# Local attention with a gated convolution: the first half pair divided behind its values, its queries and keys in four loads

## The chip, the core and the metric

The kernel runs on one core of a Trainium2 chip. Five engines work side by side, each through its own list in order: TensorE (PE, matrix products; PEld is its loading of weights), VectorE (DVE), ScalarE (ACT), GpSimd (POOL) and SyncE (SP), which here issues all transfers. The metric is device time in microseconds, the median of several runs; a profile shows one execution, with a span (first to last instruction) inside that execution's time.

## The reference

Attention within chunks of 64 positions, 8 heads of 64, then a gate: a causal convolution of five taps over the result, a sigmoid, times a projection, and a second projection.

```
scores = (q_c @ k_c.T) / 8                      # per chunk of 64
attn = exp(scores - max); attn = attn / (sum(attn) + 1e-9)
x = (attn @ v_c)  -> (8, 576, 512)
gate = sigmoid(sum over k of conv_w[k] * x shifted by 4 - k)
out = (gate * (x @ w_val)) @ w_out
```

All is 32 bits wide: q, k, v are 8 x 8 x 576 x 64, the two weights 512 x 512.

## The kernel before, in words

The 4608 positions are cut into 9 groups of 512 (g = 0 to 8). The 8 heads of a group are two pairs (p = 0, 1) of four heads each. A pair's scores are 64 small products of TensorE (`S`), into one bank of its accumulators; VectorE takes the max of each row (`mx`) and subtracts it (`sb`), ScalarE takes the exponential (`ex`), VectorE the sum and its reciprocal (`sm`), GpSimd divides (`nm`), TensorE transposes (`T`), ScalarE copies (`ec`), TensorE multiplies with the values (`A`), and ScalarE copies the result, x, with channels as partitions (`xc`). Pair 1 of group 0 has its max subtracted by TensorE (`mh`, `ml`, `sp`, then `ep`), and some pairs let ScalarE subtract it (`ng`, `ea`, `rc`).

x is then split in a rounded part (`xr`) and a residual (`xd`), so that three fast products make one exact enough (`V`, for 4 blocks m of outputs and 4 quarters c of the inputs). The weights are split likewise on the chip: they come as bits, and clamp, scale, sign, merge, shift, add, round and residual are the pieces `w1`, `w2`, `w3`, `w4`, `w5`, `w7`, `w6`, `wb` for the value weights `v` and the output weights `o`. The first products of group 0 use unsplit weights and x (`F`, two slow passes each). The taps are `k0` and `k` (VectorE mostly), the gate `sg`, its product `gm` or `vc` and `gs`, the split of it `gr` and `gd`, the second projection `P`, the copy out `oc`, the store `st`.

The order of everything is one written list, `ORDER`: a piece a word, `name group ...`. Each engine runs its share of this list in that order. A letter behind a name puts a piece on another engine (D VectorE, G GpSimd). `SLOTS` gives each tile its buffer: `ld` has six for q, k and v, `acc` four (raw weights and convolution sums), `ps` and `big` the accumulators. A piece waits for the last reader of its buffer.

Pair 0 of group 0 is in `BY_HALF`: its heads go in two halves (the third number, 0 or 1), so that the second half's scores run while the first is in the softmax. Before, the whole q and k of that pair are loaded in two transfers of 512 KB, and the division of each half (`nm 0 0 0`, `nm 0 0 1`) stands on GpSimd ahead of the half's transposes. `W` is a run of products with a zero tile, whose result nobody reads.

Of the kernel before, what the change touches and what calls it, by code (L numbers as in the profile page):

```python
# [16 lines left out]

ORDER = """lk 0 0,lq 0 0,lc,lw v 0,zr 0,w1G c 0,zw,lk 0 1,S 0 0 1,mx 0 0 1,S 0 0 0,zi,sb 0 0 1,mx 0 0 0,ex 0 0 1,zr 1,lq 0 1,
w5 v 0,sb 0 0 0,lw v 2,W 5,sm 0 0 1,w1G v 0,nm 0 0 1,w3 c 0,zm,ex 0 0 0,w5 c 0,S 0 1 0,w2 v 0,sm 0 0 0,lv 0 0,S 0 1 1,
w3 v 0,lw v 1,mx 0 1,w3 v 2,lk 1 0,nm 0 0 0,w1G v 2,w5 v 2,w2 c 0,hl 0,lq 1 0,w4 v 0,w4 c 0,T 0 0 0,w7 v 0,ec 0 0 0,  # L20
T 0 0 1,w1 v 1,mh 0 1,w9,A 0 0 0,w2 v 2,xc 0 0 0,lw o 3,w3 v 1,ml 0 1,w2 v 1,sp 0 1,ep 0 1,F 0 2 0,lw v 3,ec 0 0 1,
w4 v 2,lq 1 1,w4 v 1,k0 0 0,w7G v 2,w6 v 2,F 0 3 0,F 0 1 0,sm 0 1,w5 v 1,w7G v 1,A 0 0 1,lv 0 1,S 1 0 0,w1G v 3,
xc 0 0 1,w3G o 3,k 0 0 1,w6 v 0,nmD 0 1,lk 1 1,S 1 0 1,F 0 0 0,T 0 1,mx 1 0,k0 0 1,w5 o 3,F 0 1 1,lw o 0,w5 v 3,
w3 v 3,w1G o 3,F 0 3 1,sb 1 0,ec 0 1,ex 1 0,wb v 2,A 0 1,w2 v 3,k 0 0 4,k 0 0 2,xc 0 1 1,sm 1 0,w1G o 0,xc 0 1 0,
S 1 1 0,w3 o 0,lk 2 0,lq 2 0,xr 0 1,nm 1 0,S 1 1 1,F 0 2 1,k0 0 2,lw o 2,xn 0 1,xe 0 1,mx 1 1,sb 1 1,F 0 0 1,ex 1 1,
w4 v 3,V 0 2 2,V 0 1 2,w7G v 3,k 0 2 3,w5 o 0,sm 1 1,S 2 0 0,S 2 0 1,w3G o 2,w2 o 3,w6 v 3,T 1 0,w6 v 1,ec 1 0,mx 2 0,
V 0 0 2,lk 2 1,V 0 3 2,lq 2 1,lv 1 0,wb v 3,k 0 2 2,lv 1 1,S 2 1 0,sb 2 0,k 0 0 3,S 2 1 1,w2 o 0,ex 2 0,mx 2 1,nm 1 1,
A 1 0,V 0 0 3,k0 0 3,V 0 3 3,xr 1 0,sm 2 0,wb v 0,xc 1 0 1,sb 2 1,vc 0 3,V 0 1 3,V 0 2 3,xc 1 0 0,T 1 1,w1G o 2,
xd 1 0,ex 2 1,V 1 3 0,ec 1 1,sm 2 1,lk 3 0,lq 3 0,vc 0 1,S 3 0 0,S 3 0 1,nm 2 0,k 0 1 2,lw o 1,w2 o 2,wb v 1,A 1 1,
sg 0 0,nm 2 1,xc 1 1 0,V 1 3 1,mx 3 0,lv 2 0,gm 0 0,V 1 1 0,xc 1 1 1,hl 1,lk 3 1,ng 3 0,k 0 2 1,w1G o 1,lk 4 0,  # L30
V 1 1 1,V 1 2 0,xr 1 1,V 1 2 1,xd 1 1,V 1 3 2,w4 o 2,V 1 2 2,V 1 1 2,V 1 3 3,k 0 3 2,V 1 1 3,k 0 2 4,w4 o 0,k 0 1 3,
ea 3 0,k 0 3 4,k 0 1 1,w2 o 1,vc 1 3,T 2 1,lq 3 1,w3G o 1,T 2 0,vc 1 1,rc 3 0,k 0 3 3,w4 o 1,ec 2 0,V 1 0 0,V 1 0 1,
ec 2 1,w5 o 1,S 3 1 0,S 3 1 1,k 0 3 1,A 2 0,V 1 0 2,V 1 2 3,sg 0 2,w5 o 2,k 0 1 4,lq 4 0,mx 3 1,xr 2 0,vc 1 2,w7G o 1,
lv 2 1,sb 3 1,lq 4 1,ex 3 1,V 1 0 3,sg 0 3,k0 1 1,A 2 1,xd 2 0,w4 o 3,V 2 2 0,V 2 3 0,vc 1 0,xc 2 0 0,xc 2 0 1,lq 5 0,
w7 o 0,V 2 3 1,V 2 0 0,gm 0 2,V 2 2 1,V 2 0 1,xr 2 1,lv 3 1,lk 4 1,S 4 0 0,k0 1 2,nm 3 0,sm 3 1,S 4 0 1,gs 0 3,w6 o 1,
xd 2 1,gr 0 2,V 2 2 2,mx 4 0,k0G 1 0,sg 0 1,w7G o 2,k 1 1 3,V 2 0 2,V 2 0 3,w6 o 2,gr 0 0,gs 0 1,gdD 0 0,xc 2 1 0,
xc 2 1 1,sb 4 0,V 2 3 2,w6 o 0,V 2 1 0,w7G o 3,V 2 1 1,w6 o 3,k 1 0 1,S 4 1 0,nm 3 1,S 4 1 1,mx 4 1,k 1 0 4,gr 0 1,
gd 0 2,T 3 1,k 1 1 1,V 2 1 2,k 1 2 2,lv 3 0,vc 2 0,ec 3 1,wb o 0,ng 4 1,wb o 1,k 1 1 4,gdD 0 1,V 2 2 3,lk 5 1,k0 1 3,
k 1 2 3,V 2 1 3,P 0 2 0,vc 2 2,wbD o 2,P 0 1 0,hl 2,k 1 2 1,vc 2 1,k 1 0 3,V 2 3 3,k 1 3 4,k 1 1 2,k 1 3 1,P 0 0 0,
ea 4 1,P 0 0 1,rc 4 1,P 0 2 1,lq 5 1,vc 2 3,P 0 2 2,lk 5 0,P 0 0 2,wbD o 3,k 1 3 3,ex 4 0,T 3 0,k 1 2 4,P 0 1 1,  # L40
ec 3 0,P 0 3 0,A 3 1,k 1 3 2,A 3 0,P 0 3 1,xr 3 1,gr 0 3,k 1 0 2,xr 3 0,xc 3 0 0,sm 4 0,P 0 3 2,xc 3 0 1,P 0 1 2,
gd 0 3,sg 1 3,xcD 3 1 0,P 0 1 3,P 0 0 3,P 0 2 3,xc 3 1 1,sg 1 0,P 0 3 3,xd 3 0,oc 0 1,S 5 0 0,S 5 0 1,oc 0 0,oc 0 2,
xd 3 1,oc 0 3,S 5 1 0,S 5 1 1,V 3 3 0,gs 1 0,V 3 0 0,V 3 2 0,nm 4 1,gr 1 0,k0G 2 2,V 3 0 1,V 3 0 2,V 3 3 1,V 3 2 1,
V 3 0 3,sg 1 2,mx 5 0,V 3 3 2,mx 5 1,V 3 1 0,V 3 1 1,sb 5 0,k0 2 3,nm 4 0,T 4 0,ng 5 1,V 3 2 2,k0 2 1,V 3 2 3,V 3 3 3,
sg 1 1,ea 5 1,T 4 1,vc 3 0,vc 3 3,ec 4 0,gs 1 1,gr 1 1,gd 1 0,P 1 3 0,hl 3,lk 6 0,P 1 2 0,V 3 1 2,k 2 3 2,k 2 2 1,
V 3 1 3,k 2 1 3,lq 6 0,gs 1 2,gr 1 2,k0 3 1,lv 5 0,S 6 0 0,S 6 0 1,ec 4 1,k0G 2 0,k 2 2 2,k 2 0 4,lv 5 1,gs 1 3,
k 2 2 4,lv 4 0,gr 1 3,k 2 0 1,st 0 0,k 2 3 4,vc 3 2,lk 7 1,lv 4 1,vc 3 1,A 4 0,k 2 0 3,P 1 0 0,k 2 1 1,k 2 3 1,rc 5 1,
gdD 1 1,k 2 0 2,P 1 1 0,k 2 1 2,k 2 1 4,k 2 2 3,k0 3 3,sg 2 0,mx 6 0,P 1 2 1,k0 3 0,ex 5 0,k 2 3 3,gd 1 3,k0 3 2,
P 1 0 1,gd 1 2,P 1 1 1,P 1 3 1,sm 5 0,P 1 0 2,sg 2 1,P 1 1 2,nm 5 1,sg 2 2,P 1 2 2,sg 2 3,xr 4 0,gs 2 0,P 1 0 3,
sb 6 0,xd 4 0,k 3 0 2,gs 2 1,P 1 3 2,P 1 1 3,lq 6 1,lk 6 1,P 1 2 3,xc 4 0 0,xc 4 0 1,S 6 1 0,S 6 1 1,oc 1 2,k 3 2 1,  # L50
oc 1 0,k 3 0 1,gr 2 1,gr 2 0,A 4 1,V 4 2 0,nm 5 0,P 1 3 3,xr 4 1,ocD 1 1,V 4 0 0,k 3 3 4,V 4 2 1,st 0 2,hl 4,mx 6 1,
# [607 lines left out]
```

## Time and profile before

| | us |
|---|---|
| median of 3 runs (lowest, highest) | 265.33 (265.31, 266.5) |
| the profiled execution | 267.69 |
| its span | 265.9 |
| busy: TensorE, VectorE, ScalarE, GpSimd | 251.2, 236.3, 188.6, 103.3 |

Busy time is an average over stages with different limits, and a product's end is modelled: a busy TensorE still may wait in it. All instructions of the kernel go through one helper, so that one source line stands for all; groups are told apart by their tiles. `big` holds scores, transposes and values, `ps` the projections, `acc` raw weights and convolution sums, `x` the attention's result, `rs` sums and reciprocals, `t` and `t2a` and so on are scratch.

### The profile page before, as it was taken

Reading aid. Unit: us, or ns where it says so; the run is one execution under the profiler, and the core shown is the slowest. Engines: PE = TensorE matmul, PEld = TensorE weight load, DVE = VectorE, ACT = ScalarE, POOL = GpSimd, SP = SyncE. Lnnn points to the kernel's source line nnn. Section 1 sums busy time; section 2 is a strip of 40 time slices with the busy share of each in tenths; the row PEclk is TensorE's granted clock in tenths of the full one; section 3 lists DMA queues with packets and bytes.
Section 4 is the critical chain, followed back from the end, with each engine's and each line's share of the span. In section 5 each row is a group of like instructions: output and inputs, shape, how many; then the busy total and the mean of one; then the engine's idle time right before and its main releaser. Section 6 shows DMA issues by size and latency. Waiting matters only on the chain. (4 is left out here: it accounts for less than half of the span.)

```text
span 265.9 us, 7860 instructions
## 1 busy us (share of the span) xinstructions
PE 251.2 (94%) x3314; PEld 213.7 (80%) x3315; DVE 236.3 (89%) x329; ACT 188.6 (71%) x440; POOL 103.3 (39%) x90
## 2 busy tenths in 40 slices
...
GB/s 226 402 416 395 360 391 273 81 147 179 212 103 147 155 218 20 262 163 78 83 198 31 247 1 188 172 79 2 2 205 192 2 41 4 197 0 0 81 276 158
DMA packets 14291, 42.47 MB, mean 160 GB/s; under 512 B 1712, under 2 KB 1712, under 8 KB 14256
## 3 DMA queue, kind: packets, MB, share of 16 engines
...
q8 instruction: 26, 0.43, 0.7%
q14 instruction: 9, 0.07, 0.1%
HBM read 32.53 MB, written 9.44 MB: 158 GB/s over the span
## 5 line engine op out<-in xcount | busy, mean ns | idle before, releaser
L158 DVE SCALAR_TENSOR_TENSOR acc<-x,cw,acc 128x516 f32<-128x516 f32 (+1 forms) x144 | 106.2, 780 | 1.2 <-ACT acc L158 0.8
L158 PE MATMUL ps<-t,v_hi 128*128 128x512 f32 x240 | 82.3, 389 | 0.0
L158 PEld LDWEIGHTS ps<-t,v_hi 128*128 128x128 f32 x240 | 45.2, 189 | 7.1 <-issue 0.2
L158 PE MATMUL ps<-t,v_lo 128*128 128x512 f32 x120 | 45.6, 380 | 0.0
L158 PE MATMUL ps<-o_hi,t 128*128 128x512 f32 x124 | 44.3, 382 | 0.1
L158 PEld LDWEIGHTS big<-ld,ld 64*64 64x64 f32 x1152 | 19.4, 139 | 12.5 <-issue 10.7
L158 PE MATMUL big<-ld,ld 64*64 64x64 f32 x1152 | 21.8, 226 | 7.6 <-DMA ld<-in_q 7.1
L158 POOL TENSOR_TENSOR t<-e_row,rs 128x1024 f32<-128x1024 f32 (+1 forms) x13 | 25.1, 1933 | 8.1 <-DVE rs L158 6.5
L158 DVE TENSOR_REDUCE mx<-big 128x16 f32<-128x1024 f32 (+1 forms) x19 | 21.8, 1153 | 7.1 <-PE big L158 6.9
L158 PEld LDWEIGHTS ps<-o_hi,t 128*128 128x128 f32 x124 | 23.4, 189 | 3.8 <-DVE t2o L158 0.5
L158 ACT COPY x<-big 128x512 f32<-128x512 f32 (+3 forms) x44 | 19.4, 497 | 9.2 <-PE big L158 5.0
L158 PEld LDWEIGHTS ps<-t,v_lo 128*128 128x128 f32 x120 | 22.7, 189 | 3.0 <-issue 0.2
L158 ACT ACTIVATE acc<-x,cw 128x516 f32<-128x516 f32 (+1 forms) x27 | 19.9, 745 | 0.1
L158 ACT ACTIVATE t<-acc 128x512 f32<-128x512 f32 (+7 forms) x35 | 15.6, 505 | 5.9 <-DVE acc L158 2.8
L158 PE MATMUL ps<-o_lo,t 128*128 128x512 f32 x52 | 19.7, 379 | 0.0
L158 ACT ACTIVATE e_row<-big,mx 128x64 f32<-128x64 f32 x64 | 19.1, 363 | 0.6 <-DVE mx L158 0.6
L158 ACT ACTIVATE e_row<-e_row 128x1024 f32<-128x1024 f32 (+1 forms) x14 | 14.0, 1012 | 7.0 <-DVE e_row L158 7.0
L158 PEld LDWEIGHTS big<-t,ld 64*64 64x64 f32 x960 | 15.8, 135 | 3.9 <-issue 1.8
L158 PE MATMUL big<-t,ld 64*64 64x64 f32 x960 | 17.5, 220 | 1.0 <-issue 0.7
L158 ACT ACTIVATE t<-big 128x1024 f32<-128x1024 f32 x13 | 13.4, 1035 | 7.0 <-PE big L158 6.9
L158 DVE TENSOR_REDUCE rs<-e_row 128x16 f32<-128x1040 f32 (+1 forms) x15 | 17.4, 1157 | 0.2
L158 ACT CAST t<-big 128x1024 fp32r<-128x1024 f32 x16 | 16.5, 1033 | 1.2 <-PE big L158 1.2
...
## 6 DMA issues: line engine op xcount, KB each, us to landing
...
```

The source lines that it names most:

```text
L158: return tc.keep_in_program_order(fn(*args, **kwargs))
```

## The change

- q and k of the first pair come in four transfers of 256 KB, `lq 0 0 0`, `lk 0 0 0`, `lq 0 0 1`, `lk 0 0 1`, with weights and values between them.
- For this pair `ex` writes to the tile that the transposes read, so transposes and values work on undivided exponentials. `sm` adds 1e-9 itself. A new piece `R` multiplies the reciprocals, each repeated over 64 columns, with the identity and so spreads them over the layout of x, in the bank of the half's values; `rb` copies them out on ScalarE; and `xc` becomes a product on VectorE. `nm 0 0 0` and `nm 0 0 1` are gone.
- The list is laid anew. Up to the second projection of group 2 nearly everything moves; behind it the order of pieces stays, and only engines change. Over the whole list: four sign passes `w3` go from VectorE to GpSimd, three clamps `w1` from GpSimd to VectorE, one `w7` and one `wb` to GpSimd; of the first taps `k0` six more run on VectorE, four fewer on GpSimd and two fewer on ScalarE; one division goes from GpSimd to VectorE; two `gd`, two `oc`, two `xc` and one `ec` leave VectorE. `W` runs 4 + 2 products, not 5. The buffers in `SLOTS` are other ones, in the same number.

```diff
-ORDER = """lk 0 0,lq 0 0,lc,lw v 0,zr 0,w1G c 0,zw,lk 0 1,S 0 0 1,mx 0 0 1,S 0 0 0,zi,sb 0 0 1,mx 0 0 0,ex 0 0 1,zr 1,lq 0 1,
...
+ORDER = """lq 0 0 0,zi,lk 0 0 0,zw,S 0 0 0,hl 0,mx 0 0 0,zr 1,lq 0 0 1,lw v 0,w3G v 0,lv 0 0,sb 0 0 0,ex 0 0 0,w1 v 0,W 4,
+sm 0 0 0,w2 v 0,T 0 0 0,lk 0 0 1,zm,lw v 1,ec 0 0 0,w4 v 0,S 0 0 1,w5 v 0,lc,lw v 2,A 0 0 0,mx 0 0 1,R 0 0 0,W 2,
...
     def ex(g, p, b=None):
         e = probs[g, p][:, :, 0:D]
-        if b is not None:
-            e = half_rows(e, b)
-        run(S.activation, out=e, in_=e, func=AF.Exp, scale=SCALE)
+        if b is None:
+            run(S.activation, out=e, in_=e, func=AF.Exp, scale=SCALE)
+            return
+        if (g, p) not in normed:
+            normed[g, p] = tile_of("en", [P, 16, D], F32)
+        run(S.activation, out=half_rows(normed[g, p], b), in_=half_rows(e, b), func=AF.Exp, scale=SCALE)
...
         if b is not None:
-            r, e = r.rearrange("p (h b c) -> p h b c", h=2, b=2)[:, :, b], half_rows(e, b)
+            r, e = r.rearrange("p (h b c) -> p h b c", h=2, b=2)[:, :, b], half_rows(normed[g, p], b)
         run(V.tensor_reduce, out=r, in_=e, op=ALU.add, axis=AX.X)
+        if b is not None:
+            run(V.tensor_scalar, out=r, in0=r, scalar1=1e-9, scalar2=None, op0=ALU.add)
         run(V.reciprocal, out=r, in_=r)
...
+    def rt(g, p, b):
+
+        r, at = rss[g, p].rearrange("p (h b c) -> p h b c", h=2, b=2), x_ps[g, p, b]
+        for u in range(2):
+            for a in range(2):
+                for h in range(2):
+                    run(E.matmul, at[h * D:(h + 1) * D, u, 1, a].rearrange("p w k -> p (w k)"),
+                        lhsT=r[:, h, b, 2 * a + u:2 * a + u + 1].broadcast_to([P, D]), rhs=ident, start=False, stop=True,
+                        skip_group_check=True)
+
+    def rb(g, p, b):
+
+        wide_r[b] = tile_of("gate", [P, T], F32)
+        run(S.copy, out=in_halves(wide_r[b]), in_=half_x(g, p, b, 1))
+
...
         if (g, p) in BY_HALF:
             (col, _, _), = parts(g)
-            run(copy, out=in_halves(x_of(g)[:, 2 * p + u, col:col + T]), in_=half_x(g, p, u))
+            run(V.tensor_tensor, out=in_halves(x_of(g)[:, 2 * p + u, col:col + T]), in0=half_x(g, p, u), in1=in_halves(wide_r[u]),
+                op=ALU.mult)
             return
```

On SP's queue, from the first load on, before (`ld` tiles hold q, k, v; `acc` the raw weights):

```order
L158 DMA ld_71<-in_k 128x1024
L158 DMA ld_73<-in_q 128x1024
L158 DMA raw_cw<-in_moe_conv_w 128x40
L158 DMA acc_77<-in_moe_w_val 128x1024
L158 DMA ld_83<-in_k 128x1024
L158 DMA ld_129<-in_q 128x1024
L158 DMA acc_134<-in_moe_w_val 128x1024
L158 DMA ld_175<-in_v 128x1024
L158 DMA acc_195<-in_moe_w_val 128x1024
```

and now:

```order
L159 DMA ld_71<-in_q 128x512
L159 DMA ld_77<-in_k 128x512
L159 DMA ld_71<-in_q 128x512
L159 DMA acc_103<-in_moe_w_val 128x1024
L159 DMA ld_107<-in_v 128x1024
L159 DMA ld_77<-in_k 128x512
L159 DMA acc_131<-in_moe_w_val 128x1024
L159 DMA raw_cw<-in_moe_conv_w 128x40
L159 DMA acc_157<-in_moe_w_val 128x1024
L159 DMA ld_188<-in_k 128x1024
L159 DMA ld_190<-in_q 128x1024
```

The keys and queries of pair 1 (`ld_83`, `ld_129`; now `ld_188`, `ld_190`) stood fifth and sixth; now they are tenth and eleventh, behind the values and two more quarters of the value weights.

On TensorE, behind the warming products, before (`big_155` are the scores of pair 1, `ps_264` and so on sums of the first products, `t_221` the copied transposes):

```order
L158 MATMUL big_155<-ld_83,ld_129 64x64 x32
L158 MATMUL ps_215<-ident,t_147 128x128 x4
L158 MATMUL ps_223<-ident,t_147 128x128 x4
L158 MATMUL big_233<-t_221,ld_175 64x64 x16
L158 MATMUL big_155<-mh_230,minus 128x512
L158 MATMUL big_155<-ml_256,minus 128x512
L158 MATMUL big_155<-mh_230,minus 128x512
L158 MATMUL big_155<-ml_256,minus 128x512
L158 MATMUL ps_264<-x_209,t_193 128x512
```

and now (`big_252` are the scores of pair 1, `big_159` and `big_230` the values of half 0 and 1 with their spread reciprocals `rs_119`):

```order
L159 MATMUL ps_203<-ident,t_110 128x128 x4
L159 MATMUL ps_228<-x_97,t_105 128x512
L159 MATMUL big_230<-t_133,ld_107 64x64 x16
L159 MATMUL big_252<-ld_188,ld_190 64x64 x32
L159 MATMUL big_230<-ident,rs_119 64x128 x8
L159 MATMUL ps_311<-x_97,t_105 128x512
L159 MATMUL ps_316<-x_97,t_105 128x512
L159 MATMUL big_252<-mh_307,minus 128x512
```

Pair 1's scores stood ahead of half 0's transposes; now they stand behind the first product and half 1's values, with half 1's spreading and two products between them and the subtraction of their max.

## Rows read from the trace of the kernel before

**Rows 1.** Windows, whole run: length, busy of each engine (xcount), PEclk, DMA share, GB/s.

```profile
6.70:75.00 68.30, 62.91 (x1197) 49.40 (x1191) 64.47 (x90) 57.38 (x123) 47.19 (x38) 1.00 0.76 288
75.00:241.00 166.00, 166.00 (x1990) 145.07 (x1989) 162.73 (x227) 122.90 (x306) 51.90 (x41) 1.00 0.32 108
```

**Rows 2.** Chain of waits, last long piece: start us, us, what.

```profile
241.16 21.00 PE ps L158 x96
```

**Rows 3.** Timeline, head: start, us, engine, operation, tiles, count [idle before <-releaser].

```profile
5.53 1.99 PE L158 MATMUL big<-ld,ld 64*64 64x64 f32 x64 [5.53 <-DMA ld<-in_q]
...
6.72 0.69 DVE L158 TENSOR_REDUCE mx<-big 128x8 f32<-128x512 f32 x1 [5.61 <-PE big L158]
...
8.17 0.63 ACT L158 ACTIVATE e_row<-e_row 128x512 f32<-128x512 f32 x1 [6.17 <-DVE e_row L158]
...
10.88 1.16 PE L158 MATMUL big<-ld,ld 64*64 64x64 f32 x64 [1.54 <-DMA ld<-in_q]
...
12.73 1.09 PE L158 MATMUL ps<-ident,t 128*128 128x128 f32 x8 [0.69 <-POOL t L158]
...
15.67 2.74 PE L158 MATMUL ps<-x,t 128*128 128x512 f32 x6
```

**Rows 4.** Timeline, pair 1 of group 0, ScalarE and then TensorE.

```profile
15.89 1.01 ACT L158 ACTIVATE e_row<-big 128x1024 f32<-128x1024 f32 x1
...
25.90 1.03 ACT L158 CAST t<-big 128x1024 fp32r<-128x1024 f32 x1
...
28.01 0.79 PE L158 MATMUL ps<-t,v_hi 128*128 128x512 f32 x1
```

**Rows 5.** Timeline of TensorE, three stalls and the second checkpoint.

```profile
35.94 0.81 PE L158 MATMUL big<-t,ld 64*64 64x64 f32 x39 [0.73 <-issue]
...
43.33 1.16 PE L158 MATMUL big<-t4b,ld 64*64 64x64 f32 x64 [0.92 <-issue]
44.42 0.48 PE L158 MATMUL ps<-t,v_hi 128*128 128x512 f32 x1
...
64.89 0.50 PE L158 MATMUL big<-ld,ld 64*64 64x64 f32 x17 [0.50 <-issue]
```

**Rows 6.** Windows of the head, for the loads: the last number is GB/s.

```profile
3.00:3.75 0.75, 0.00 (x0) 0.00 (x0) 0.00 (x0) 0.00 (x0) 0.00 (x0) 1.00 1.00 393
...
5.25:6.00 0.75, 0.47 (x17) 0.50 (x21) 0.00 (x0) 0.00 (x0) 0.21 (x1) 1.00 0.50 175
...
10.00:15.00 5.00, 3.18 (x105) 2.77 (x106) 4.61 (x12) 2.91 (x9) 3.14 (x5) 1.00 1.03 419
```

**Rows 7.** Groups by form on VectorE: busy us, mean ns | idle before.

```profile
L158 DVE TENSOR_TENSOR t<-e_row,rs 128x1024 f32<-128x1024 f32 x2 | 2.4, 1218 | 0.0
...
L158 DVE TENSOR_SCALAR t<-acc 128x512 uint32<-128x512 uint32 x3 | 1.5, 508 | 0.0
...
L158 DVE TENSOR_SCALAR acc<-x,cw 128x512 f32<-128x512 f32 x2 | 1.0, 476 | 0.0
...
L158 DVE COPY t<-ps 128x512 f32<-128x512 f32 x1 | 0.7, 678 | 0.0
```

**Rows 8.** Groups by form on GpSimd.

```profile
L158 POOL TENSOR_TENSOR t<-t,t 128x512 uint32<-128x512 uint32 x2 | 3.6, 1818 | 3.3 <-DVE t L158 2.0 <-ACT t L158 1.3
...
L158 POOL TENSOR_TENSOR t<-e_row,rs 128x512 f32<-128x512 f32 x2 | 2.2, 1136 | 1.6 <-DVE cw_h L158 1.6
...
L158 POOL TENSOR_SCALAR t2a<-acc 128x512 uint32<-128x512 f32 x1 | 2.0, 1995 | 0.1
```

**Rows 9.** Windows from stall to stall, for the counts of PE and PEld.

```profile
35.93:43.32 7.39, 6.47 (x126) 5.29 (x126) 6.69 (x9) 6.46 (x11) 7.07 (x6) 1.00 0.81 304
43.32:64.88 21.56, 21.07 (x382) 18.15 (x381) 19.68 (x28) 19.97 (x58) 14.24 (x11) 1.00 0.50 173
```

**Rows 10.** The page, DMA queues: packets, MB, share of 16 engines.

```profile
q8 instruction: 26, 0.43, 0.7%
```

**Rows 11.** Timeline of VectorE, one wait.

```profile
46.63 1.23 DVE L158 TENSOR_TENSOR t<-big,t 128x1024 fp32r<-128x1024 f32 x1 [1.38 <-ACT t L158]
```

More of the change, by code (lines that the diff above doesn't have):

```diff
@@ new lines @@
+T 6 0,k 4 1 4,oc 2 1,V 5 0 0,xc 5 1 1,V 5 3 1,V 5 0 1,k0 5 1,gr 3 2,oc 2 3,gs 3 3,V 4 3 0,sm 6 1,gs 3 0,st 1 2,
+k0D 5 2,ec 6 0,S 7 0 0,S 7 0 1,k 4 1 3,oc 2 2,nmD 6 1,mx 7 0,A 6 0,st 0 1,V 5 1 0,sb 7 0,V 5 0 2,V 5 1 1,gd 3 2,
+V 5 1 2,V 5 1 3,gr 3 0,st 1 3,k 4 2 3,gr 3 3,V 4 3 1,V 4 3 2,V 5 0 3,k 4 0 1,gd 3 3,vc 5 1,k 4 1 2,V 5 3 2,ex 7 0,
+gdD 3 1,k 5 1 2,k 4 3 1,vc 5 0,lv 7 0,V 4 3 3,k 4 2 1,lk 8 1,k0 5 3,V 5 3 3,gd 3 0,vc 5 3,vc 4 3,k 5 0 1,xr 6 0,
+P 3 2 0,P 3 1 0,k 5 1 1,k 4 1 1,P 3 3 0,k 4 3 4,sg 4 2,P 3 3 1,xd 6 0,sg 4 1,xc 6 0 0,xc 6 0 1,k 5 2 1,T 6 1,k 5 2 3,
```

172 lines of the change are left out of this document (85 added, 87 removed).

## The prediction, before the changed kernel had run

> **What bounds the kernel now.** I read the sums by stage first, then the head in order of time, then the waits without a releaser. From 75 to 241 us TensorE is busy 166.00 of 166.00 us and VectorE 162.73 [rows 1]: there is no room on TensorE behind 75 us, and VectorE has 3.3 us of it. From 6.7 to 75 us TensorE lacks 5.4 of 68.3 us. So the change pays only by how far TensorE is when it enters the long stretch, if VectorE comes along. After its last wait the chain is TensorE alone, 96 products in 21.00 us [rows 2]: 0.22 each, 0.66 for a piece of three.
>
> The head [rows 3]: the first scores start at 5.53, when two loads of 512 KB are in. Max, subtraction, exponential, division on GpSimd, transposes (12.73), values and a copy follow, and at 15.67 the first product of x and the value weights, two passes of 0.43 each. Beside it pair 1 of group 0 starts its scores at 10.88, and its chain is the longer one: exponential 15.89, rounding 25.90, first rounded product 28.01 [rows 4]. I use 28.01 as first checkpoint, and as the second 44.42 [rows 5], where the values of pair 1 of group 1 have ended.
>
> **The loads.** Scores of half 0 need 512 KB instead of 1 MB. At 393 GB/s [rows 6] that is 1.33 us less: start at 4.2. Four half loads are two issues more on SP's queue, which the transfers outlast. Three more 512-KB loads (values, two quarters of the value weights) stand ahead of pair 1's queries than before: at 419 GB/s [rows 6] 1.25 us each, 3.75 together, so its scores start at 14.6, not at 10.88. The queries of pair 1 go into the tile of half 0's and half 1's keys, so SP waits for the second score run (9.0), with all later loads behind it; the queues then still hold three loads (3.75 us), and nothing runs dry. A lull of 175 GB/s [rows 6] lies behind the tap load; I let it move with that load, still ahead of pair 1. If it goes, pair 1's loads are up to 1.4 us earlier (two such slices, estimated), of which 0.8 remains, because VectorE would then wait for GpSimd's sign pass of weights 2 before pair 1's max.
>
> **Half 0, step by step.** Durations are those of [rows 3, 7, 8]; a ScalarE pass of 512 is 0.63 throughout. Max at 4.2 + 1.19 = 5.4; it and the subtraction 0.69 each, exponential 0.63: 7.45. Four transposes, half of 1.09 and its latency, 0.65, on undivided numbers; copy behind two small passes of ScalarE: 9.15. Values 0.65: 9.8. VectorE meanwhile sums (0.69), adds 1e-9 and inverts: both are not shown at this size alone; above 0 and below the 0.69 of a 512 pass, I take 0.35 for both: 8.5, which leaves 1.3 us of cover. Spreading the reciprocals is new: 16 passes of 128 columns, each a quarter of the 0.43 pass, 0.107: 1.7 us in a row, 0.86 if two halves of the array run together, as the 64 small passes of [rows 3] do (1.16 / 64 = 0.018 each). I take 0.9, nearer that row. Copy, then the product on VectorE (0.69): x at 12.0. Weights: GpSimd's sign pass 2.0 from 6.0, VectorE's merge until 9.25, GpSimd's addition 1.8 from 9.85: 11.65. So the first product comes at 12.1 instead of 15.67, 3.6 us earlier. GpSimd loses two divisions (1.14 each).
>
> New waits: ScalarE's copy of the reciprocals holds the exponential of half 1 until 11.3, and a pass over weights 2, due at 11.9, holds half 1's copy; its values end at 14.0. Both are covered, since TensorE's next work, pair 1's scores, waits for data until 14.6.
>
> **Why little of the 3.6 us remains.** From 14.6: scores 1.16, max (1.22) done at 17.05; the max is spread over the scores behind half 1's reciprocals and two products (0.9 + 1.7): 19.2. On ScalarE two weight roundings stand ahead: exponential 19.5 to 20.5. VectorE is free at 20.5 too (a merge, a product, three taps). Sum and reciprocal 1.5, division 1.2: transposes 23.2, copied 25.1, values end 26.2. ScalarE runs the next exponential (1.0) before the rounding: 27.6. With the correction and one product 28.9 at the first checkpoint: 0.9 late. Its third matmul needs the residual, which now stands behind two copies and a tap: 30.5.
>
> From there: two pieces; transposes 31.4 (GpSimd has divided by 30.2); scores 33.4; two pieces 34.7; scores 35.7; two pieces 37.0; values 38.05; a piece; transposes 39.6; three pieces 41.6; scores 42.65; values 43.7. Before, that is 44.42, with a piece (0.66) less done. The change is ahead by 0.7 + 0.66 = 1.35, and only because two stalls are missing from my line.
>
> **The stalls.** Before, TensorE stops for 0.73 until 35.94, 0.92 until 43.33 and 0.50 until 64.89, and nothing in the profile releases it [rows 5]. Between the first two it runs 126 + 126 instructions, to the third 382 + 381, three times 254 [rows 9]; the instruction queue moved 26 transfers, 0.43 MB [rows 10]. I read them as blocks of code that come late where 64-pass runs take a block in 2 us. The Trainium skill (Runtime: NRT & Kernel Launch, "Instruction fetch mechanics") has blocks of 256 instructions too, which agrees, but calls the cost of a crossing "mostly hidden"; here three crossings show 0.50 to 0.92. By that page the stalls would have another cause and stay in the change: then 2 x 0.8 comes back, and the time is that of rival 2.
>
> Counted in the order, the changed program has 32 to 66 TensorE instructions more before the same work, so the first two boundaries lie earlier: one inside the second scores of group 2, which slow pieces now precede, one ahead of the first scores of group 3, with five slow steps in front. I cost them at 0, bounds 0 and 2 x 0.92. A later boundary falls between scores and values that stand back to back: 0.7 against the 0.50 of before.
>
> **VectorE.** Removed: four sign passes (0.51), an addition and a weight residual (0.69 each), two residuals and two copies (0.68), a copy of 1.22, two smaller ones to x (0.8, estimated from the 0.68): -8.2. Added: six taps (0.48), a division (1.22), two products (0.69), two clamps of 0.5 at most and a small one (1.1), the small adds 0.3: +6.9. Net -1.3 [rows 7]. Up to 40 us I count equal work and equal idle time: it starts 1.3 earlier and waits 1.0 for the sign pass and the late scores. Behind that it waited 1.38 for ScalarE at 46.63 [rows 11], after the second stall; that goes with the stall. So it can follow by 1.4 us.
>
> **Sum.** -1.35 at 44 us, -0.50 + 0.7 later, 0 in the last 21 us: -1.1 (rounded). The profiled execution took 267.69 (span 265.9), so 266.6; the median of the three runs is 265.33, 2.36 below it, and on that footing the forecast is 264.2.
>
> **Rivals.** Rival 1, more gain: no stall of code up to 75 us, and the lull goes: -1.35 - 0.5 - 0.8 = -2.65, 262.7. For it: most crossings of the long stretch cost nothing, since TensorE is busy there throughout. Against it: the queues are full until 40 us, where code must come through.
>
> Rival 2, no change: two stalls come back at new places, 0.73 + 0.92: +0.55, 265.9. For it: exactly those full queues.
>
> Rival 3, the clock. The granted clock is 1.00 in every row (the 2.4 GHz level), yet the first 64 score passes took 1.99 us and the run at 10.88 took 1.16 [rows 3]. TensorE is less filled between 10 and 14.6 than before; if pair 1's scores and one product run at the slow pace again, that is 0.83 + 0.86: +0.6, 265.9. The Trainium skill (TensorE: Matmul & The Clock Gate, "What's actually happening") says the throttled state is the default and activity releases it; the pause of 1.5 us ahead of 10.88 did not bring it back here.
>
> Rival 4, slower: GpSimd becomes the bound. It takes four sign passes of 2.0 and an addition of 1.8 and gives up two half divisions and two cheaper clamps (0.7, estimated at a third of the sign pass): some 6 us more work before 47 us [rows 8]. My line has no cover in two places: the addition for weights 1 ends at 21.4 and two products must fit before 23.2; the first whole division must end by 31.4. If it is 1.1 late at the first and group 2's divisions 1.8 late, the change stands at -1.1 + 2.9 = +1.8, 267.1. It decides from the point where the first division ends behind 31.4. Against it: GpSimd starts 2 us earlier, and group 2's divisions have 4 us of cover in my line.
>
> **How the numbers follow.** Forecast 0.50, own range 262.9 to 265.6; rival 1 0.15, rival 2 0.10, rival 3 0.07, rival 4 0.18. Within 0.5%, which is 1.33 us and about what a measurement can tell, reaches down to 264.0: the forecast's half splits into 0.25 faster and 0.25 same. Faster 0.25 + 0.15 = 0.40, same 0.25 + 0.17 = 0.42, slower 0.18. The range for 8 in 10 takes in the stalls' and the lull's bounds and leaves out half of rival 4 and the far end of rival 1: 262.2 to 267.2.
>
> **What would show it.** Right: first scores at 4.2, first product near 12.1, pair 1's scores at 14.6 after a wait for a load, its exponential at 19.5, first checkpoint at 28.9. Pair 1's scores before 13: the loads are mis-sized. TensorE waiting for GpSimd's divisions: rival 4. Waits without a releaser above 0.5 us, 254 instructions apart: rival 2. Wrong altogether if VectorE's residual of group 1 comes over 1 us after 39.6, or if TensorE has new idle time behind 75 us.

## The result, and the profile after

The changed kernel takes 269.35 us (median of 4 runs, 268.83 to 270.3), the kernel before 265.32. The ratio is 1.0145, with a 95% interval of 1.0104 to 1.0186: 3.9 us slower. I had forecast 264.2 and a range up to 267.2; it is slower, by more than I gave to any rival.

The profiled execution took 270.3, its span 268.5, so from profile to profile the loss is 2.6 us. The rest is the footing: the profiled execution of before lay 2.36 above its median, this one 0.95.

Windows of the profile after (length, busy of PE, PEld, DVE, ACT, POOL, then PEclk, DMA share, GB/s), to be read against [rows 1]:

```profile
6.70:75.00 68.30, 61.96 (x1215) 47.95 (x1214) 62.60 (x86) 56.38 (x119) 50.60 (x38) 1.00 0.78 281
75.00:241.00 166.00, 165.96 (x1993) 145.08 (x1992) 163.01 (x228) 125.35 (x310) 50.29 (x40) 1.00 0.33 113
241.00:268.50 27.50, 23.77 (x111) 20.47 (x109) 10.55 (x15) 8.37 (x15) 2.93 (x2) 1.00 0.33 125
```

From 75 to 241 nothing changed: TensorE is full in both. The loss is made before 75 us and shows at the end. TensorE was busy 0.95 us less up to 75 (61.96 against 62.91), although it had some 2 us more to do there: the spreading, 2 x 1.09. The 23.77 us behind 241 were 21.00 before [rows 2].

The head on TensorE in the timeline (start, us, engine, operation, tiles, count, idle before and what ended it), against [rows 3, 4]:

```profile
4.67 1.13 PE L159 MATMUL big<-ld,ld 64*64 64x64 f32 x32 [4.67 <-DMA ld<-in_k]
...
10.56 0.69 PE L159 MATMUL big<-ld,ld 64*64 64x64 f32 x32 [1.43 <-DMA ld<-in_k]
...
11.65 1.09 PE L159 MATMUL big<-ident,rs 128*64 128x128 f32 x16
...
14.45 1.02 PE L159 MATMUL ps<-x,t 128*128 128x512 f32 x2
15.41 0.69 PE L159 MATMUL big<-t,ld 64*64 64x64 f32 x32
16.58 1.16 PE L159 MATMUL big<-ld,ld 64*64 64x64 f32 x64 [0.48 <-DMA ld<-in_q]
...
26.07 1.06 PE L159 MATMUL big<-ident,t 128*128 128x128 f32 x8 [0.56 <-DVE t L159]
...
31.52 0.73 PE L159 MATMUL big<-t,minus 128*128 128x512 f32 x2 [1.18 <-ACT x L159]
...
32.55 0.79 PE L159 MATMUL ps<-t,v_hi 128*128 128x512 f32 x1
```

In order: the first scores (5.53 before), half 1's scores behind a wait for their keys, the spreading of half 0, the first product (15.67 before), half 1's values, pair 1's scores (10.88 before), pair 1's transposes, its correction, and the first checkpoint (28.01 before). Half 0 won 1.2 us at its first product; pair 1's scores lost 5.7, and 4.54 of that is still there at the checkpoint.

Windows of the loads (as above, GB/s last), against [rows 6]; the lull is earlier, longer and deeper:

```profile
3.25:5.75 2.50, 1.08 (x33) 1.00 (x34) 0.00 (x0) 0.00 (x0) 0.00 (x0) 1.00 0.65 134
```

VectorE, ScalarE and GpSimd, timeline rows of pair 1 and one of group 1:

```profile
24.19 1.73 DVE L159 TENSOR_TENSOR t<-e_row,rs 128x1024 f32<-128x1024 f32 x1
...
30.38 1.08 ACT L159 COPY x<-big 128x512 f32<-128x512 f32 x2
...
31.15 1.91 POOL L159 TENSOR_TENSOR t<-e_row,rs 128x1024 f32<-128x1024 f32 x1 [0.43 <-DVE rs L159]
```

Pair 1's division took 1.73, not the 1.22 of [rows 7]. The two copies stand between pair 1's rounding and its correction, which waits for them (the 1.18 above). GpSimd's first whole division waits for VectorE's reciprocals: GpSimd is not the bound.

The second checkpoint on TensorE, against [rows 5]:

```profile
47.99 1.16 PE L159 MATMUL big<-t4b,ld 64*64 64x64 f32 x64 [1.26 <-ACT t2p L159]
49.09 0.48 PE L159 MATMUL ps<-t,v_hi 128*128 128x512 f32 x1
```

It comes 4.67 late (44.42 before), with one piece (0.66) more done than before at this point; with that piece counted, as the prediction did, it is 4.0 late. The pause of 1.26 is charged to a pass of ScalarE (`t2p`, from 47.28), but it is no wait for that pass: with one tile of the loads changed (the first experiment) the same products start at 46.51 and that pass at 46.67. It fits the load of the values that they read, issued at 40.12, which took (DMA of the window 40.1 to 40.5: KB, us to landing)

```profile
ld<-in_v SPq DMA_DIRECT2D x1, 512.0 KB, 7.7
```

and so landed at 47.8. In the run with passes in the changed kernel's own pause (below) the profile itself charges 0.64 at this place to that load. Pauses like those of [rows 5], which nothing in the profile releases, do not appear on TensorE in the changed kernel's profile.

### The profile page after: what moved, and what is told of

Read it like the earlier page. It is cut to its first block, busy times and chain, and to the rows that moved or that the text cites. A ratio compares the mean times of both kernels' runs of the same rounds, so it can differ in the third digit from the quotient of the medians.

```text
span 268.5 us, 7941 instructions
## 1 busy us (share of the span) xinstructions
PE 253.7 (94%) x3348; PEld 214.9 (80%) x3348; DVE 237.3 (88%) x329; ACT 191.4 (71%) x444; POOL 104.6 (39%) x88
## 4 chain that ended last, share of the span: by engine, by line
PE 83%; POOL 5%; DMA 5%; DVE 3%; issue 1%; ACT 1%; SPq 1%; POOLq 0%; ACTq 0%
PE ps L159 67%; PE big L159 16%; DMA ld<-in_k 3%; POOL t L159 2%; DMA ld<-in_q 2%; POOL v_lo L159 1%; DVE rs L159 1%; SPq L159 1%; POOL t2i L159 1%; POOL t2o L159 1%; DVE t L159 1%; DVE e_row L159 0%; DVE mx L159 0%; ACT e_row L159 0%; POOL t2l L159 0%
## 5 line engine op out<-in xcount | busy, mean ns | idle before, releaser
L159 PE MATMUL ps<-t,v_hi 128*128 128x512 f32 x224 | 78.0, 390 | 0.0
L159 PEld LDWEIGHTS ps<-t,v_hi 128*128 128x128 f32 x224 | 42.2, 189 | 6.9 <-issue 0.2
L159 PE MATMUL ps<-o_hi,t 128*128 128x512 f32 x108 | 39.7, 384 | 0.0
L159 POOL TENSOR_TENSOR t<-e_row,rs 128x1024 f32<-128x1024 f32 x14 | 28.0, 2002 | 10.1 <-DVE rs L159 10.1
L159 POOL COPY x<-x 128x16 f32<-128x16 f32 x8 | 3.4, 423 | 54.9 <-DVE acc L159 40.3
L159 PEld LDWEIGHTS ps<-o_hi,t 128*128 128x128 f32 x108 | 20.4, 189 | 2.9
L159 ACT COPY t<-ps 128x512 f32<-128x512 f32 x22 | 13.1, 602 | 6.0 <-PE ps L159 5.7
L159 PEld LDWEIGHTS big<-ident,t 128*128 128x128 f32 x128 | 14.7, 141 | 3.2 <-ACT t2c L159 1.4
L159 PE MATMUL big<-ident,t 128*128 128x128 f32 x128 | 16.4, 273 | 0.6 <-DVE t L159 0.6
L159 DVE TENSOR_TENSOR e_row<-big,mx 128x1024 f32<-128x1024 f32 (+1 forms) x14 | 16.1, 1147 | 0.8
```

The costliest lines, as they stand in the source:

```text
L159: return tc.keep_in_program_order(fn(*args, **kwargs))
```

## The experiments

Each ran beside the kernel before on its chip; ratios are to those runs of before. Pieces are written as in the order: a name with its group, pair or chunk, and half. The edits are cut: they show the pieces that move and their neighbours, not whole lines of the list, and where a tile's buffer in `SLOTS` had to follow, that is left out.

**Pair 1's queries in a tile of their own** (on the changed kernel).

```diff
-    ld="213015201342135231053144
+    ld="213045201342135231053144
```

> The changed kernel, with pair 1's queries in a tile of their own, so that their load is queued right behind the load of pair 1's keys and no longer waits for the second half's scores (they started at 16.58 in the changed kernel, its queries landed 2.05 us behind its keys). Theory 1 (the late loads of pair 1 set the first rounded product, 32.55, and all behind it): the queries land 0.8 earlier, pair 1's scores start near 15.8, the whole 0.8 shorter, 268.5 us. Theory 2 (the spreading's 2.05 us on TensorE and its copies cost the time): no change, 269.3. If nothing moves although the scores start earlier, something behind the scores (VectorE, GpSimd) is the longer chain.

Measured: 270.78, ratio 1.0164 (1.0103 to 1.0226). No gain. Timeline rows of TensorE, then a window of its own (PEclk third from the end):

```profile
11.42 1.97 PE L159 MATMUL big<-ident,rs 128*64 128x128 f32 x16
...
16.06 0.69 PE L159 MATMUL big<-t,ld 64*64 64x64 f32 x32
16.57 1.11 PE L159 MATMUL big<-ld,ld 64*64 64x64 f32 x64
```

```profile
9.90:13.40 3.50, 3.48 (x81) 3.05 (x82) 2.45 (x5) 0.27 (x1) 2.24 (x5) 0.58 1.03 406
```

Pair 1's scores no longer wait for a load, but start at 16.57 all the same, right behind half 1's values, which stand in front of them on TensorE; and half 0's spreading took 1.97 here instead of 1.09, at a granted clock of 0.58, mostly the lower level (1.2 GHz). In the changed kernel the two limits, half 0's chain (16.1) and the load (16.4), lie within half a microsecond of each other, so that freeing one alone brings little.

**Pair 1 first in the queue** (on the changed kernel).

```diff
+lq 0 0 1,lk 0 0 1,lw v 0,lk 0 1,lq 0 1,lv 0 0
+S 0 0 1,S 0 1 0,S 0 1 1
+ec 0 0 1,ep 0 1
+F 0 3 0,sp 0 1
+xc 0 0 1,sm 0 1,nmD 0 1
```

> The changed kernel, with pair 1's keys and queries ahead of the values and of two quarters of the weights in the load queue, its queries in a tile of their own, and its scores, max and checkpoint pieces written that much earlier. Theory 1: pair 1's scores start near 12.4 instead of 16.58, half 0's first product falls back to about 16.5, the first rounded product comes near 28.4 instead of 32.55, and the time loses 3.5 of the 4.0 us: 265.8. Theory 2: the spreading is still there and the time stays above 268. Theory 3 (GpSimd's four sign passes are late): the first rounded product stays above 31 with a wait for GpSimd in front.

Measured: 273.04, ratio 1.0232 (1.0167 to 1.0297). In this kernel pair 1's exponential comes ahead of the subtraction of its max, which then has no effect. Timeline rows of TensorE and VectorE:

```profile
10.52 1.16 PE L158 MATMUL big<-ld,ld 64*64 64x64 f32 x64 [1.02 <-DMA ld<-in_q]
...
19.30 1.09 PE L158 MATMUL big<-ident,rs 128*64 128x128 f32 x16
...
35.03 1.33 PE L158 MATMUL ps<-t,v_hi 128*128 128x512 f32 x1
```

```profile
21.29 0.68 DVE L158 TENSOR_TENSOR x<-big,t2a 128x512 f32<-128x512 f32 x1
...
23.43 2.10 DVE L158 TENSOR_TENSOR t<-e_row,rs 128x1024 f32<-128x1024 f32 x1
```

The scores start at 10.52, as in before, and the division at 23.43, only 0.8 earlier than in the changed kernel: I had written it behind half 1's product (21.29), which needs the reciprocals that TensorE spreads from 19.30 on. The checkpoint comes at 35.03, 2.5 later than in the changed kernel. An early start is not enough.

**Copies ahead of the rounding** (on the changed kernel).

```diff
-xr 0 1,xc 0 1 1
+xc 0 1 1,xc 0 1 0,xr 0 1
```

> The changed kernel, with the two copies of pair 1's x ahead of its rounding on ScalarE. In the changed kernel the correction, which overwrites the bank that the copies read, waited for them (1.18 us until 31.52), and the first rounded product came behind it. Theory 4 (this order is a term of its own): the rounding ends 0.6 to 1.0 later, the correction starts 0.5 earlier at most, and the first rounded product comes 0 to 0.6 us earlier; the time is 268.7 to 269.3. Theory 1 alone: no change within 0.3.

Measured: 269.56, ratio 1.0120 (1.0068 to 1.0171): no change. TensorE's correction in the timeline:

```profile
31.66 0.73 PE L159 MATMUL big<-t,minus 128*128 128x512 f32 x2 [1.18 <-ACT t L159]
```

The same wait, now for the rounding: all three passes of ScalarE must end first. Their order is not a cause.

**The division alone, in the order of before** (VectorE's product for half 1 ahead of pair 1's division).

```diff
-nm 0 0 1
-nm 0 0 0
+A 0 0 0,R 0 0 0,rb 0 0 0
+A 0 0 1,R 0 0 1,rb 0 0 1
```

> The kernel before with its own order and whole loads, but with the changed division alone: the first half pair's division behind its values, the reciprocals spread by 2 x 16 passes on TensorE and copied by ScalarE, and VectorE's product in place of the copies of x. Theory 2: the spreading costs what the change lost, 2 us on TensorE and two copies of 0.63 on ScalarE ahead of pair 1's exponential: 267.5 to 269. Theory 1: TensorE has idle time in front of pair 1's correction, which hides most of it: 265.0 to 266.3, and the first rounded product stays within 1 us of 28.01.

Measured: 269.61, ratio 1.0133 (1.0076 to 1.0189). Timeline rows of VectorE:

```profile
21.58 0.69 DVE L158 TENSOR_TENSOR x<-big,wide 128x512 f32<-128x512 f32 x1 [2.30 <-ACT wide L158]
...
22.85 1.66 DVE L158 TENSOR_TENSOR t<-e_row,rs 128x1024 f32<-128x1024 f32 x1
```

VectorE waits 2.30 for the spread reciprocals with pair 1's division queued behind. That is either the spreading's price or that of this place, so the next run moves one piece.

**The same, half 1's product behind pair 1's division.**

```diff
-lv 0 1,S 1 0 0,w1G v 3,xc 0 0 1
+k 0 0 1,w6 v 0,nmD 0 1,xc 0 0 1
```

> The kernel before with the changed division in its own order and loads (as in the run where VectorE waited 2.30 us for the spread reciprocals of half 1 with pair 1's division queued behind), but the product for half 1 now stands behind pair 1's division on VectorE. Theory B: VectorE's wait goes, pair 1's division starts near 19.3 (19.04 before, 22.85 in that run), the first rounded product comes within 1 us of 28.01, and the time is 265 to 266.5. Theory C: 2 x 1.03 us of spreading and the two copies stay on the way, and the time stays at 267.5 or above. Theory A says as B, since pair 1's scores start near 10.5.

Measured: 267.32 over 10 runs, ratio 1.0052 (1.0020 to 1.0083), which is 1.4 us. Timeline rows of VectorE and TensorE:

```profile
19.79 1.22 DVE L158 TENSOR_TENSOR t<-e_row,rs 128x1024 f32<-128x1024 f32 x1
...
21.57 0.69 DVE L158 TENSOR_TENSOR x<-big,wide 128x512 f32<-128x512 f32 x1 [0.57 <-ACT wide L158]
```

```profile
13.18 1.09 PE L158 MATMUL big<-ident,rs 128*64 128x128 f32 x16
...
19.76 1.09 PE L158 MATMUL big<-ident,rs 128*64 128x128 f32 x16
...
29.81 0.80 PE L158 MATMUL ps<-t,v_hi 128*128 128x512 f32 x1
```

The place was worth 2 us; the rest is the division itself: it delays the checkpoint by 1.80 and the end by 1.4, of the 2.2 us that it adds to TensorE. Both theories had asked for another number; it lies between them.

**Pair 1's loads late, nothing else** (on the kernel before).

```diff
-lw v 0,zr 0,w1G c 0,zw,lk 0 1
+lw v 0,zr 0,w1G c 0,zw,lw v 2,lv 0 0,lw v 1,lk 0 1
```

> The kernel before, with nothing changed but the load queue: the values of pair 0 and two quarters of the weights stand ahead of pair 1's keys and queries, as in the changed kernel. Pair 1's scores then start near 14.6 instead of 10.88. Theory A (each microsecond by which pair 1's scores are late comes back at the first rounded product and at the end, whatever the division does): first rounded product 31 to 32 instead of 28.01, time 268.3 to 269. Theory B (VectorE's order around the new division is what costs): the late scores are covered by other work, time below 266.5. Theory C (the spreading on TensorE costs its 2 us): as B, since nothing is spread here.

Measured: 271.64, ratio 1.0194 (1.0126 to 1.0263). TensorE in the timeline:

```profile
14.12 1.99 PE L158 MATMUL big<-ld,ld 64*64 64x64 f32 x64 [4.27 <-DMA ld<-in_q]
16.04 1.84 PE L158 MATMUL ps<-ident,t 128*128 128x128 f32 x8
...
31.72 0.79 PE L158 MATMUL ps<-t,v_hi 128*128 128x512 f32 x1
```

The order of the loads alone costs as much as the whole change, or more. In the profiled execution, with 269.59 the quickest of the four, the scores are late by 3.24 and the checkpoint by 3.71; the passes right behind the pause ran at half pace (1.99 and 1.84; 1.16 and 1.09 in [rows 3]).

**The same, with TensorE kept busy through the pause.**

```diff
-W 5
+W 20
```

> The kernel before with pair 1's loads late, as in the run that took 271.6, and with 20 passes over the constant tile on TensorE in place of 5, which fill its pause of 4.27 us ahead of pair 1's scores. If the half pace behind the pause is part of the cost, pair 1's scores take 1.16 instead of 1.99 and the transposes 1.09 instead of 1.84, the first rounded product comes near 30.2 instead of 31.72, and the time is 269 to 270.5. If the lateness alone costs (theory A in its plain form), 271 to 272.

Measured: 269.3 over 10 runs, ratio 1.0102 (1.0075 to 1.0129), 2.7 us. TensorE in the timeline:

```profile
7.59 5.14 PE L158 MATMUL ps<-warm 128*128 128x512 bf16 x20
13.95 1.16 PE L158 MATMUL big<-ld,ld 64*64 64x64 f32 x64 [1.22 <-DMA ld<-in_q]
15.04 1.09 PE L158 MATMUL ps<-ident,t 128*128 128x128 f32 x8
...
30.73 0.80 PE L158 MATMUL ps<-t,v_hi 128*128 128x512 f32 x1
```

Full pace, and 2.4 us less by the ratios, though the two intervals just touch. Scores late by 3.07 make the checkpoint late by 2.72 and the end by 2.7: nearly all of it comes through.

**Both parts together** (division as in the 267.3, loads as in the 271.6).

```diff
+lw v 0,zr 0,w1G c 0,zw,lw v 2,lv 0 0,lw v 1,lk 0 1
+A 0 0 0,R 0 0 0,rb 0 0 0
+nmD 0 1,xc 0 0 1
```

> The kernel before with two parts of the change together and its own order otherwise: the division behind the values with spread reciprocals (product for half 1 behind pair 1's division, 267.3 alone) and pair 1's keys and queries behind the values of pair 0 and two quarters of the weights (271.6 alone). Theory E (the change is these two parts, and they overlap, since TensorE waits for pair 1's load while it spreads): 269 to 271, first rounded product near 32. If they simply add: 272.9. If the division takes the load's place as the limit: 267.5 to 268.5.

Measured: 272.67, ratio 1.0237 (1.0178 to 1.0297). Timeline rows of TensorE, then a window of it (busy, then PEclk) over its first passes behind the pause:

```profile
14.92 1.99 PE L158 MATMUL big<-ld,ld 64*64 64x64 f32 x64 [5.39 <-DMA ld<-in_q]
...
35.55 0.79 PE L158 MATMUL ps<-t,v_hi 128*128 128x512 f32 x1
```

```profile
14.90:19.60 4.70, 4.68 (x105) 0.53 1.03 419
```

At the end the parts add: 0.0052 + 0.0194 is 0.0246. At the checkpoint they do not: it comes 7.54 late, where the two single profiles give 1.80 + 3.71; 0.8 of that is a later start of the scores than with late loads alone (14.12). The half pace is in it, here with a granted clock of 0.53, nearly the level of 1.2 GHz.

**Four loads, nothing else** (on the kernel before), **and with the division.**

```diff
-lk 0 0,lq 0 0
+lk 0 0 1,lq 0 0 1,lk 0 0 0,lq 0 0 0
```

> The kernel before with only the first pair's queries and keys in four loads of 256 KB, second half first, as its scores want them. Before, the transfers slowed down between 4.5 and 6.0, behind 1.05 MB; in the changed kernel between 3.25 and 5.75, behind 0.52 MB; both are 256 rows of the tiles, and there the tap load came 5 us later. If the slowdown follows the number of rows, it comes at 3.25 here, the second half pair of loads lands near 7 instead of 5.39 and the second scores wait for it, while pair 1's queries still land near 10.7 and the time stays within 0.3% of before: 264.6 to 266. If the slowdown followed the tap load, it would come at 4.5 again, with nothing late. First scores near 4.5 in both cases.

> The kernel before with the division behind the values (267.3 alone) and the first pair's queries and keys in four loads (no change alone), in the order of before. Theory E: the four loads cost and bring nothing here either: 266.8 to 267.8. If the earlier first scores pay once GpSimd's division is gone from behind them: below 266.5.

Measured: 266.39, ratio 0.9998 (0.9969 to 1.0027); with the division 268.4, ratio 1.0076 (1.0045 to 1.0107). A window and TensorE's rows of the first:

```profile
3.25:5.75 2.50, 1.00 1.00 235
```

```profile
4.13 1.14 PE L159 MATMUL big<-ld,ld 64*64 64x64 f32 x32 [4.13 <-DMA ld<-in_q]
6.74 1.13 PE L159 MATMUL big<-ld,ld 64*64 64x64 f32 x32 [1.47 <-DMA ld<-in_q]
```

The scores start 1.4 earlier, and what is won goes to the wait for the other half. The lull came early although the tap load kept its place behind the four: it does not follow the tap load. The 268.4 lies above the 267.8 that I had written, but 1.0076 and the 1.0052 of the division alone lie in each other's intervals; its profile has pair 1's scores and the transposes at half pace (1.99 and 1.97).

**Whole loads in the changed kernel.**

```diff
-lq 0 0 0,zi,lk 0 0 0
+lq 0 0,zi,lk 0 0
```

> The changed kernel with the first pair's queries and keys in two whole loads again, all else as it is. First scores at 5.5 instead of 4.67; the second half's scores wait for no load (they waited 1.43 us in the changed kernel and started at 10.56) and start near 9; the load of pair 1's queries, which waits for them, is issued near 10 instead of 11.30 and lands near 15 instead of 16.44. Theory A: pair 1's scores start near 15.3 instead of 16.58, and the time is 268.2 to 268.8. Theories B and C: no change, 269.3 or more.

Measured: 269.32, ratio 1.0105 (1.0071 to 1.0140). First scores at 5.48, yet half 1's began at 9.91 at half pace, so the load of pair 1's queries, which waits for them, was issued at 11.1 (11.3 in the changed kernel) and its scores began at 17.21. Theory A's number fell with its condition. As far as the time tells, the four loads neither cost nor bring anything here.

**Pair 1 put back, and then group 1 too** (on the changed kernel).

```diff
+S 0 0 1,S 0 1 0,S 0 1 1
+mx 0 1,mh 0 1,ml 0 1,sp 0 1,W 2
+ex 0 0 1,ep 0 1
+sm 0 0 1,sm 0 1
+rb 0 0 1,xc 0 0 1,nmD 0 1
+F 0 0 0,S 1 0 0,S 1 0 1,T 0 1,ec 0 1
```

> The changed kernel (four loads, division behind the values, spreading on TensorE, all of it), but with pair 1 put back to where the kernel before has it: its keys and queries are loaded right behind half 1's keys and one quarter of the weights, its scores stand ahead of half 0's values on TensorE, its max correction ahead of half 0's first product, its exponential behind half 1's on ScalarE, its sum behind half 1's on VectorE and its division behind the product for half 1, its transposes ahead of the weight products of half 1. Theory A (the late start of pair 1 is what the change lost): its scores start near 10.5 instead of 16.58, its transposes near 21.5 instead of 26.07, the first rounded product comes at 28.5 to 30 instead of 32.55, and the time is 265.5 to 267.5, of which about 1.3 us is the spreading as the run of the division alone had it. If instead something that came with the new order behind 30 us is the cause, the first rounded product comes early and the time stays above 268.5.

> The run with pair 1 put back, taken one step further: group 1's first max and subtraction stand directly behind pair 1's division on VectorE (three taps and a merge of weights were in front; 27.31 there, 20.17 in the kernel before), its exponential ahead of pair 1's rounding on ScalarE, its sum and division earlier, and pair 1's correction and first weight products directly behind two products of half 1. Theory D (in that run, and in the changed kernel, the order on VectorE and ScalarE behind the first pair is a limit of its own, beside the scores' start): group 1's max near 23.5, the transposes of group 1 without the wait of 1.21 for GpSimd's division, first rounded product near 30, time 267 to 269. If the time stays at 271, the loss is not in this order.

Measured: 271.17, ratio 1.0182 (1.0156 to 1.0208), and 271.93, ratio 1.0221 (1.0174 to 1.0268). Timeline rows of the first, VectorE and then TensorE:

```profile
21.04 0.69 DVE L159 TENSOR_TENSOR x<-big,t2a 128x512 f32<-128x512 f32 x1 [0.75 <-ACT t2a L159]
21.65 1.71 DVE L159 TENSOR_TENSOR t<-e_row,rs 128x1024 f32<-128x1024 f32 x1
```

```profile
11.11 1.16 PE L159 MATMUL big<-ld,ld 64*64 64x64 f32 x64 [1.14 <-DMA ld<-in_q]
...
31.96 0.80 PE L159 MATMUL ps<-t,v_hi 128*128 128x512 f32 x1
...
36.02 1.33 PE L159 MATMUL big<-ident,t 128*128 128x128 f32 x7 [1.21 <-POOL t L159]
```

and of the second, TensorE and then ScalarE:

```profile
30.29 0.80 PE L159 MATMUL ps<-t,v_hi 128*128 128x512 f32 x1
...
36.60 0.62 ACT L159 CAST v_hi<-t2b 128x512 fp32r<-128x512 f32 x1 [3.65 <-POOL t2b L159]
```

Early scores (11.11) again brought little: VectorE now waits for the spread reciprocals, and pair 1's division starts at 21.65 (19.04 in before). In the second kernel the checkpoint came at 30.29, but the weights became late, as their passes had been put behind pair 1's and group 1's. Theory D failed in its number: each place taken back in this order cost something elsewhere. An early checkpoint with a time above 268.5 is also what I had written for a cause behind 30 us in the new order; these two runs do not exclude it.

**The spreading twice** (on the changed kernel).

```diff
+R 0 0 0,R 0 0 0
+R 0 0 1,R 0 0 1
```

> The changed kernel with each half's spreading pass run twice on TensorE (the reciprocals add up, so the first pair's x is doubled: the output is not the reference's). This adds 2 x 1.03 us of TensorE ahead of half 0's first product and ahead of pair 1's max correction, and nothing to any other engine. If TensorE's order is tight there (pair 1's scores waited only 0.48 for their load behind half 0's work), pair 1's scores start 0.5 later, its correction 1.0 to 1.6 later, and the time is 270.3 to 271.4. If the spreading is covered by waits, 269.3 to 269.8.

Measured: 276.82 (275.63 to 279.18), ratio 1.0430 (1.0358 to 1.0501). The second half's passes took 1.97, pair 1's scores began at 18.03 and the checkpoint came at 35.31, 2.76 late for some 2.2 us of passes, part of them at half pace: nothing covers the spreading. That the end is 7.5 late is far beyond my number; pauses without a releaser are part of it, one of 1.64 in TensorE's timeline, and the rest is not settled.

```profile
52.64 0.33 PE L159 MATMUL big<-t4b,ld 64*64 64x64 f32 x3 [1.64 <-issue]
```

**Passes in the changed kernel's own pause.**

```diff
-T 0 0 0,lk 0 0 1
+T 0 0 0,W 13,lk 0 0 1
...
-        for _ in range(n):
+        for _ in range(n % 9):
```

(`W 13` stands for four more products, in the accumulator of the first run of `W`.)

> The changed kernel with four more passes over the constant tile on TensorE behind half 0's transposes, in the pause of 1.43 us ahead of half 1's scores. If the changed kernel too loses by the half pace in some of its executions (half 0's spreading took 1.97 instead of 1.09 in one run at a granted clock of 0.58), the median falls to 268.3 to 269. If not, 269.0 to 269.6, since the four passes end before the keys land.

Measured: 269.01 over 10 runs, ratio 1.0106 (1.0078 to 1.0134). That is on the border of my two numbers and inside the interval of the changed kernel: whether the pace there costs anything stays undecided, and at most a part of the loss is it. The first checkpoint on TensorE:

```profile
31.56 0.79 PE L159 MATMUL ps<-t,v_hi 128*128 128x512 f32 x1
```

It comes 1.0 earlier than in the changed kernel, whose work up to there is the same but for the four passes: so far apart can single profiles lie.

**Pair 1's loads one earlier** (on the kernel before).

```diff
-lw v 0,zr 0,w1G c 0,zw,lk 0 1
+zr 0,w1G c 0,zw,lk 0 1
-lq 0 1,w5 v 0
+lq 0 1,lw v 0
```

> The kernel before with pair 1's keys and queries one load earlier, ahead of the first quarter of the weights (whose clamp, rounding and scaling are written behind half 0's exponential and division). Pair 1's queries land near 9.5 instead of 10.74. Theory A in its plain form (the time follows pair 1's load, microsecond for microsecond) says 1.2 us less: 264. With VectorE as the limit in front of pair 1's max (it was busy without a pause from 6.72 to 11.8 and waited only 0.32 for the scores), at most 0.3 is to be had: first rounded product 27.7 to 28.0, time 265.0 to 265.5, or later if the first weights, 2.5 us late, hold half 0's first product.

Measured: 267.78, ratio 1.0059 (1.0038 to 1.0080). The first quarter of the weights is used here before it is scaled. TensorE's transposes waited 1.98 for GpSimd's division, the checkpoint came at 29.77. My rearrangement of the weight passes delayed half 0, so it says nothing of the limit.

## Why the prediction was wrong

**Where the loss comes from.** Put into the kernel before one at a time, two parts of the change each cost something clear of noise: the division a ratio of 0.0052 (0.0020 to 0.0083), the late loads at full pace 0.0102 (0.0075 to 0.0129). Together that is 0.0154; the change has 0.0145 (0.0104 to 0.0186). So the loss has the size of these two parts, to within about a microsecond. At the checkpoint they make 1.80 + 2.72 = 4.52, and the changed kernel's is 4.54 late; that this fits so closely is luck, since single profiles lie 1.0 apart and the run with both parts was 2.0 over its own sum. That these two parts are the cause in the changed kernel is argued, not shown. There half 0's chain holds pair 1's scores as long as the load does (16.1 against 16.4), so the part that I call late loads is there the late start from either. And taking the lateness out of the changed kernel did not win it back in three tries: VectorE's division then stands behind half 1's product, and even where the checkpoint came earlier, at 30.29 with pair 1 and group 1 put back, the time was 271.93. What the rest of the new order costs by itself was not tested. Whether some other order would do better is open; no version here beat the kernel before.

**"So its scores start at 14.6, not at 10.88."** This is the first term that was mis-sized: 16.58. The queries landed at 16.4, 1.8 later than I said. I let the lull move with the tap load, and it came 1.25 us earlier instead and lasted 2.5; and the tile shared with half 1's keys made the issue wait until those scores were done (11.3), where I had written 9.0.

**"Both are covered, since TensorE's next work, pair 1's scores, waits for data until 14.6."** I cost the spreading nearly right (0.9 a half; 1.09 in the rows) and counted half 1's on pair 1's path, but half 0's chain, with its own spreading in it, I set to nothing. It was not covered: half 1's scores waited 1.43 for their keys, the values and the spreading stood behind them, half 0's first product came at 14.45, not 12.1, and half 1's values ended at 16.1, not 14.0.

**"28.9 at the first checkpoint: 0.9 late."** This is the step that failed. I had 3.7 of delay at the scores shrink to 0.9. Pair 1's chain carried it through (3.07 to 2.72 in the run with only that; 5.70 to 4.54 in the changed kernel), and behind the scores the changed kernel needed 15.97 where I had 14.3: the division at 1.73 and the copies ahead of the correction, which I placed behind the rounding without seeing that the correction overwrites what they read. With the 2.0 by which the scores start later than 14.6, these 1.7 make up the distance from 28.9 to 32.55.

**"The change is ahead by 0.7 + 0.66 = 1.35, and only because two stalls are missing from my line."** The measured difference at the second checkpoint is +4.67, or +4.0 with the piece counted. The two stalls did stay away, as I had cost them, and the later one that I had put at 0.7 did not come either; it did not help. From the first checkpoint to the second I had 14.8 and it took 16.54, and 1.26 of that is the pause at the values, which fits their load: a wait that my line did not have. The footing may count the stalls a second time. I took two of them out of an execution that lay 2.36 above its median, and then took off the 2.36 too; the kernel before with four loads, profiled at 265.71, has one such pause (0.85) and not three. No profile of a median execution of before shows it. On "mostly hidden" (the Trainium skill, Runtime: NRT & Kernel Launch, "Instruction fetch mechanics") the runs show both, three pauses in the profile of before and none in that of the changed kernel; that the pauses are fetches of code was not tested.

**The rivals.** Rival 4 had the sign and the wrong engine: GpSimd waited for VectorE. Its time of 267.1 was also too low. Rival 3, the clock, came true in the wrong kernel: the changed one shows 1.00, but the late loads alone cost 2.4 us more with the pause than without it. Behind a wait of 5.39 the granted clock was 0.53, and behind 20 passes the pace was full. That agrees with the Trainium skill (TensorE: Matmul & The Clock Gate, "What's actually happening"), by which the throttled state is the default and activity releases it. Rival 2's stalls did not come, and neither did rival 1's gain.

**What was right.** That the change pays only by TensorE's position when it enters the long stretch, that nothing is lost or won behind 75 us, and that half 0 is not the longer chain. From the last of these I should have started: a change that delays the longer chain by three loads to shorten the other is slower unless that chain has slack, and I found slack for it that I had not measured.
